# The inverse stage in float32 on quarters of the array, and spectra of batch 1 held back behind it

## The chip, the cores and the metric

One core of one Trainium2 chip runs the kernel. The time is that of the device, in microseconds, from one launch. Only TensorE multiplies matrices; VectorE, ScalarE and GpSimd work element by element; SyncE (SP) and the other engines' queues start DMAs. An engine takes its instructions in the order in which they stand in its list and waits at each for what it needs.

## The reference

The input x is 4 batches of 3072 tokens with 256 channels. Three layers follow one another:

```python
X = np.fft.rfft(x, axis=1)                       # over the tokens of a batch
Yr = Xr @ w_r - Xi @ w_i + b_r;  Yi = Xr @ w_i + Xi @ w_r + b_i
Y = soft_threshold(Yr, 0.01) + 1j * soft_threshold(Yi, 0.01)
x = np.fft.irfft(Y, n=3072, axis=1)              # 12288 tokens in all
e = argmax(x @ w_gate)                           # one of 8 experts
# in token order the first 384 tokens of an expert are kept, the rest give 0
y = gate_weight * (relu(x @ w1[e]) @ w2[e])
out = silu(y @ w_in) @ w_out                     # for the kept tokens
```

Since an expert keeps its first 384 tokens only, the kernel transforms batch 0 and the beginning of batch 1, and takes a second, longer way through all batches only where an expert is not full by then. That way is not run with these inputs.

## The kernel before, in words

The transform over 3072 tokens is done in factors of 48 and 64. For a batch `s1` multiplies by a 96 x 96 table (tile `c1f`) and writes to a scratch array `a_d`. `kphase` then runs over k = 0, 2, ..., 22, two frequencies at a time: `forward` reads rows `ar` and makes the spectrum (tile `xp`, the products that the order calls `xp<-c,ar`, then copies and differences `xk`), `shrink` multiplies by the weights (24 float32r products `yp<-wri,xk`) and applies the threshold on VectorE (`y`, `cl`, `cl`), and `back` transforms back (`bp<-cl,c`) and writes to a scratch array `b_d`. For one k, `shrink` comes one step and `back` three steps later. A float32 operand is split into a high and a low float32r part, and three float32r products (`mm3`: high by high, low by high, high by low) give nearly the float32 result.

The inverse stage `is2` reads `b_d` in 8 groups g (rows `br`), splits each row tile into `bh` and `bl`, multiplies by `c4`, copies to `ao`, writes `attn`, turns `ao` by transposes (`tp`, copied to `aT`), and multiplies by the gate's weights (`lg<-aT,wg`); after groups 3 and 7 the logits are turned (`lt`) and `choose` picks experts. `route` counts positions with VectorE passes and two small products (`bs`), makes the one-hot factors `ft` and matrices `pm`, and multiplies them (`tb<-ft,pm`) into a table of token numbers and gate weights. `rank` orders the experts by load (`key`, `rk`, `sel`, `ids`, `idi`); SP reads `idi` to load the weights (`st`) of the first experts, and `slots` makes the addresses `srcs` with which GpSimd gathers the tokens `xg`. Those are scaled by VectorE, turned (`gtp`) and split (`xT`), and then the experts' layers begin (`hp`, `y`, `h`, `o`) and run to the end; beside the first of them `third` does the inverse stage, the gate and the routing for the first third of batch 1 (`ps<-br,c4p`).

A planner with estimated costs puts each engine's list in order ahead of the run: an instruction that is written later may be moved up where its inputs would be ready. So spectra of batch 1 (`self.kphase(1, ads, True)`, written behind `is2`, `route` and `rank`) stand among the inverse stage of batch 0. `after(ins, first)` adds a wish of order to that planner: `ins` stands behind `first` on the same engine, with no semaphore. Tiles with one tag share that tag's buffers, and in PSUM, which has 8 banks, `ps` has three of them, `xp` two, and `yp`, `yq` and `bp` one each; `lg` of `is2` uses the bank `yq`.

Of the kernel before, what the change touches and what calls it, by code (L numbers as in the profile page):

```python
# [17 lines left out]
N1, N2 = 48, 64  # L18
# [18 lines left out]
HELD = 10  # L37
FULL = 0, 1, 3, 5, 7, 9, 11, 13, 15
BIG = 65536.0
UP = 65536.0  # L40
# [10 lines left out]
def _split(a):  # L51
    hi = _round12(a)
    return hi, _round12(a - hi.astype(np.float64))


def _tables():
# [23 lines left out]
    c1 = np.einsum("akr,pz->apkrz", c1, eye2).reshape(Q, Q)  # L80
    c4 = np.einsum("kra,pz->krpaz", c4, eye2).reshape(Q, Q)
    m = np.zeros((NK, 2, N2, 2, N2))
# [10 lines left out]
    for half, f0 in ((0, 0), (1, N1 // 2)):  # L93
# [22 lines left out]
    ind = ind.transpose(1, 0, 2).reshape(2, 2 * P)  # L116
    u, q = np.arange(P) // QB, np.arange(P) % QB
    at = TW * q + GT * u
# [3 lines left out]
        "c1": np.stack(_split(c1) + (c1,), 1).reshape(Q, -1),  # L122
        "c4": np.stack(_split(c4) + (c4,), 1).reshape(Q, -1),
        "tab": tab,
# [28 lines left out]
class Kernel:  # L153
    def __init__(self, ctx, tc, i, o):
# [17 lines left out]
        self.stored = {}  # L172
        self.again, self.evicted = False, None

# [208 lines left out]
    def kphase(self, b, ads, ahead=False):  # L383
# [12 lines left out]
        def spectrum(xp, ar, kq, tb):  # L396

            for c in range(2):
                nc.tensor.matmul(xp[:, c], ar[:, kq, c * P:(c + 1) * P], c2[:, tb], start=True, stop=True)

        def forward(k, ar):
            first = k == 0
            kq = k % KG
            xk = kp.tile([P, 2, 4, 192], FR, tag="xk", name="xk", bufs=3)
            xp = self.pk.tile([P, 4, P], F32, tag="xp", name="xp", bufs=self.xb)
            for j in range(2):
                spectrum(xp[:, 2 * j:2 * j + 2], ar, kq + j, k + j + 1)
            js = slice(2, 4) if first else slice(0, 4)
            up, mid, low = slice(64, 192), slice(128, 192), slice(0, 64)
            nc.scalar.copy(xk[:, 0, :, up], xp)  # L410
            v.tensor_tensor(xk[:, 1, :, up], xp, raw(xk[:, 0, :, up]), ALU.subtract)
            nc.scalar.activation(xk[:, 0, js, low], xp[:, js, 64:], AF.Copy, scale=-1.0)
            v.tensor_tensor(xk[:, 1, js, low], raw(xk[:, 0, js, mid]), xp[:, js, 64:], ALU.subtract)
            xo = None
            if first:
                xp = self.pk.tile([P, 4, P], F32, tag="xp", name="xp", bufs=self.xb)
                spectrum(xp, ar, 0, 0)
                xo = kp.tile([P, 2, 2, P], FR, name="xo", bufs=1)
                self.split("av", xo[:, 0], xo[:, 1], xp[:, :2])
            return xk, xo  # L420

        def shrink(k, xk, xo):
            yp = self.pk.tile([P, 2, D], F32, tag="yq" if k % 4 and b != 1 else "yp", name="yp", bufs=1)
            for j in range(2):
# [41 lines left out]
    def route_consts(self):  # L466
        nc, bp = self.nc, self.bc
        self.c4 = bp.tile([Q, 2, Q], FR, name="c4", bufs=1)
        t = bp.tile([Q, 3, Q], F32, name="c4f", bufs=1)
        nc.sync.dma_start(out=t, in_=self.i["c4"].rearrange("q (h m) -> q h m", h=3))  # L470
        nc.vector.tensor_copy(self.c4, t[:, 0:2])
        self.c4p = bp.tile([Q, QB], F32, name="c4p", bufs=1)
        nc.vector.tensor_copy(self.c4p, t[:, 2, 0:QB])
        kw = dict(allow_small_or_imprecise_dtypes=True)
# [38 lines left out]
    def third(self, b, res):  # L513

        nc, bp, ps, wg, CH = self.nc, self.bp, self.ps, self.wg, self.CH
        v = nc.vector
        c4 = self.c4p
        bv = self.bds[b].rearrange("k (r u g) c -> (k r) u (g c)", r=4, u=4)
        od = self.attn[0][b * S:b * S + QB * TW].rearrange("(q u g) d -> u q (g d)", u=4, g=GT)
        res[b] = self.chosen(1)  # L520
        def rows(n):
# [10 lines left out]
            for u in range(4):  # L532
                nc.sync.dma_start(out=od[u, :, n * CH:(n + 1) * CH], in_=aof[u * QB:(u + 1) * QB])
            return ao
# [29 lines left out]
    def is2(self, b, qbs, res):  # L564
# [3 lines left out]

        nc, bp, ps, c4, wg, CH, LD = self.nc, self.bp, self.ps, self.c4, self.wg, self.CH, self.LD
        v = nc.vector  # L570
        NB = len(qbs)
        q0, nq = qbs[0] * QB, NB * QB
        qs = slice(q0, q0 + nq)
        bv = self.bds[b].rearrange("k (r u g) c -> (k r) u g c", r=4, u=4)
        r0 = b * S + q0 * TW
        h = int(r0 >= NEAR)
        od = self.attn[h][r0 - h * NEAR:r0 - h * NEAR + nq * TW].rearrange("(q u g) d -> q u g d", u=4, g=GT)
        res[b] = self.chosen(NB)
# [3 lines left out]
        def rows(g):  # L582
            br = bp.tile([Q, LD], F32, tag="xt", name="br", bufs=self.sb)
            nc.sync.dma_start(out=br.rearrange("q (u c) -> q u c", c=D), in_=bv[:, :, g])
            ao = bp.tile([Q, 4, 2, P], F32, tag="ao", name="ao2", bufs=self.sb)
            aof = ao.rearrange("q u h d -> q (u h d)")
            for z in range(0, LD, CH):
                sl = slice(z, z + CH)
                bh = bp.tile([Q, CH], FR, tag="xh", name="bh", bufs=self.sb)
                bl = bp.tile([Q, CH], FR, tag="xl", name="bl", bufs=self.sb)  # L590
                self.split("av", bh, bl, br[:, sl])
                pt = ps.tile([Q, CH], F32, tag="ps", name="ps2")
                self.mm3(pt[:nq], c4[:, 0, qs], c4[:, 1, qs], bh, bl, True, True)
                nc.scalar.copy(aof[:nq, sl], pt[:nq])
            nc.scalar.dma_start(out=od[:, :, g], in_=aof[:nq].rearrange("q (u c) -> q u c", c=D))
            return ao

        def turn(ao):
            aT = bp.tile([P, 2, NB, 4, QB], F32, tag="aT", name="aT")
            for h in range(2):  # L600
                tp = ps.tile([P, 4, nq], F32, tag="ps", name="tp")
                for u in range(4):
                    nc.tensor.transpose(tp[:, u], ao[:nq, u, h], self.ident[:nq, :nq])
                v.tensor_copy(aT[:, h].rearrange("p b u q -> p u b q"), tp.rearrange("p u (b q) -> p u b q", q=QB))
            return aT

        def gate(g, aT):
# [4 lines left out]
            for h in range(2):  # L612
                for j in range(NB):
                    nc.tensor.matmul(lg[COL * j:COL * (j + 1), z], wg[:, h], aT[:, h, j].rearrange("p u q -> p (u q)"),
                                     start=h == 0, stop=h == 1)
            if z == GS - 1:
# [18 lines left out]
    def route(self, b, qbs, res):  # L635
# [466 lines left out]
```

## Time and profile before

| | |
|---|---|
| three runs | 655.97, 658.72, 662.19 us, median 658.72 |
| profiled execution | 661.11 us, its span 659.3 us |
| mean granted TensorE clock | 0.967 |
| TensorE busy | 623.8 us, 95% of the span |
| DMA | 83.1 MB, 126 GB/s over the span |

The profile is of one execution. Times of its rows count from the span's start. A TensorE row gives the start, the duration, the source line and the product, with its shape; one float32 product is recorded twice, so that x2 is one product, and a float32r product once. Durations of products overlap, so what a row of products costs is the distance from start to start. The granted clock is a share of 2.4 GHz; 0.50 is 1.2 GHz.

### The profile page before, as it was taken

Reading aid. Unit: us, or ns where it says so; the run is one execution under the profiler, and the core shown is the slowest. Engines: PE = TensorE matmul, PEld = TensorE weight load, DVE = VectorE, ACT = ScalarE, POOL = GpSimd, SP = SyncE. Lnnn points to the kernel's source line nnn. Section 1 sums busy time; section 2 is a strip of 40 time slices with the busy share of each in tenths; the row PEclk is TensorE's granted clock in tenths of the full one; section 3 lists DMA queues with packets and bytes.
Section 4 is the critical chain, followed back from the end, with each engine's and each line's share of the span. In section 5 each row is a group of like instructions: output and inputs, shape, how many; then the busy total and the mean of one; then the engine's idle time right before and its main releaser. Section 6 shows DMA issues by size and latency. Waiting matters only on the chain. (4 is left out here: it accounts for less than half of the span.)

```text
span 659.3 us, 10829 instructions
## 1 busy us (share of the span) xinstructions
PE 623.8 (95%) x4060; PEld 570.1 (86%) x4060; DVE 331.8 (50%) x673; ACT 314.8 (48%) x640; POOL 76.6 (12%) x81
## 2 busy tenths in 40 slices
PE   8699999999985999999999999999999999999993
PEld 4387889877873579899999999999999999999993
DVE  3348986667595579973423236632225632223330
ACT  4434543555331356654645445544544554544450
POOL 1001220000013211250101022000112000101001
PEclk9779999999995899999999999999999999999998
DMA  8996945893217865799600014400004400000000
GB/s 240 320 242 195 302 167 162 211 275 106 81 64 212 267 203 160 224 322 345 194 9 17 9 34 150 129 17 1 25 9 122 126 18 1 25 1 25 1 1 29
DMA packets 63542, 83.10 MB, mean 126 GB/s; under 512 B 4948, under 2 KB 53144, under 8 KB 63480
## 3 DMA queue, kind: packets, MB, share of 16 engines
q1 hardware_dynamic: 51640, 66.58, 33.3%
q10 hardware_dynamic: 9536, 9.44, 4.6%
q0 software_dynamic: 2304, 6.29, 3.0%
q8 instruction: 34, 0.56, 0.3%
q14 instruction: 28, 0.23, 0.1%
HBM read 49.79 MB, written 32.51 MB: 125 GB/s over the span
## 5 line engine op out<-in xcount | busy, mean ns | idle before, releaser
L190 DVE TENSOR_TENSOR gl<-sg,gh 128x384 fp32r<-128x384 f32 x118 | 65.5, 558 | 160.9 <-ACT gh L182 157.2
L1025 ACT ACTIVATE sg<-h 128x384 f32<-128x384 f32 x128 | 62.6, 492 | 112.2 <-PE h L200 111.4
L199 PE MATMUL o<-wo,gl 128*128 128x256 f32 x354 | 92.9, 282 | 0.0
L200 PE MATMUL o<-wo,gh 128*128 128x256 f32 x354 | 92.8, 282 | 0.0
L198 PE MATMUL h<-yT,wi 128*128 128x384 f32 x256 | 86.3, 337 | 0.4 <-ACT yT L182 0.4
L199 PE MATMUL h<-yT,wi 128*128 128x384 f32 x256 | 86.1, 336 | 0.0
L200 PE MATMUL h<-yT,wi 128*128 128x384 f32 x256 | 85.7, 337 | 0.0
L198 PE MATMUL o<-wo,gh 128*128 128x256 f32 x354 | 73.6, 282 | 0.0
L199 PEld LDWEIGHTS o<-wo,gl 128*128 128x128 f32 x354 | 67.1, 189 | 0.1
L200 PEld LDWEIGHTS o<-wo,gh 128*128 128x128 f32 x354 | 67.1, 190 | 0.0
L182 ACT CAST gh<-sg 128x384 fp32r<-128x384 f32 x118 | 60.2, 514 | 8.7 <-PE o L200 5.7
L198 PEld LDWEIGHTS o<-wo,gh 128*128 128x128 f32 x354 | 59.9, 189 | 0.0
L182 ACT CAST w<-st 128x512 fp32r<-128x512 f32 x64 | 39.2, 619 | 36.5 <-DMA st<-in_moe_w 17.9
L198 PE MATMUL yp<-wri,xk 128*128 128x256 f32 x188 | 55.2, 293 | 0.0
L190 DVE TENSOR_TENSOR w<-st,w 128x512 fp32r<-128x512 f32 x64 | 45.7, 718 | 17.9 <-ACT w L182 17.8
L199 PE MATMUL yp<-wri,xk 128*128 128x256 f32 x188 | 54.3, 289 | 0.0
L200 PE MATMUL yp<-wri,xk 128*128 128x256 f32 x188 | 53.5, 285 | 0.0
L991 ACT ACTIVATE hh<-hp 128x384 fp32r<-128x384 f32 x64 | 31.5, 492 | 41.3 <-PE y L199 19.9
L198 PEld LDWEIGHTS h<-yT,wi 128*128 128x128 f32 x256 | 48.2, 188 | 0.7 <-ACT yT L182 0.7
L199 PEld LDWEIGHTS h<-yT,wi 128*128 128x128 f32 x256 | 48.1, 188 | 0.0
L200 PEld LDWEIGHTS h<-yT,wi 128*128 128x128 f32 x256 | 48.1, 188 | 0.0
L992 DVE SCALAR_TENSOR_TENSOR hl<-hp,hh 128x384 fp32r<-128x384 f32 x64 | 35.1, 552 | 24.6 <-ACT hh L991 24.4
(224 smaller groups left out, 1255.2 us busy)
## 6 DMA issues: line engine op xcount, KB each, us to landing
st<-in_moe_w SPq DMA_DIRECT2D x64, 256.0 KB, 3.4
out<-zt SPq DMA_DIRECT2D x48, 256.0 KB, 3.6
a_d<-ao SPq DMA_DIRECT2D x16, 384.0 KB, 4.9
ar<-a_d SPq DMA_DIRECT2D x12, 512.0 KB, 5.1
b_d<-bo ACTq DMA_DIRECT2D x12, 512.0 KB, 3.0
br<-b_d SPq DMA_DIRECT2D x16, 384.0 KB, 4.7
xt<-in_x SPq DMA_DIRECT2D x15, 384.0 KB, 6.9
nt<-in_moe_w_in SPq DMA_DIRECT2D x8, 512.0 KB, 7.9
```

Source lines behind the costliest of these rows:

```text
L182: self.nc.scalar.copy(dst, src)
L190: e.tensor_tensor(dst, src, raw(hi), ALU.subtract)
L198: first = nc.tensor.matmul(out, lh, rh, start=start, stop=False)
L199: nc.tensor.matmul(out, ll, rh, start=False, stop=False)
L200: return first.ins, nc.tensor.matmul(out, lh, rl, start=False, stop=stop).ins
L991: nc.scalar.activation(hh, hp, AF.Relu)
L992: self.evicted = nc.vector.scalar_tensor_tensor(hl, hp, 0.0, raw(hh), ALU.max, ALU.subtract).ins
L1025: nc.scalar.activation(sg, hp, AF.Silu)
```

## The change

`c4` is now one float32 table: a 48 x 48 table in the partitions 0 to 47 and once more in 64 to 111, and the third's table behind it. `tiled` multiplies the two halves of the rows (parity p, 48 partitions each) by it in float32, for two column halves ch, into four quarters of the array: rows 64p, output partitions 64ch. It takes two PSUM banks, one for each p. The token order inside a group changes with it: partition and free index swap roles, so reads and writes are made of two DMAs each, `third` and the token numbers follow, and transposes are 128 wide. `gated[g]` keeps the last gate product of group g; spectra of batch 1 for k = 8 are put behind group 2, k = 10 behind group 5, and k = 12 to 22 behind group 7. In batch 1 the products `yp` for k = 14, 18 and 22 use the bank `yq`. One factor of `route` moves from GpSimd to VectorE.

```diff
+PACE = {4: 2, 5: 5, **{n: GT - 1 for n in range(6, 12)}}
...
+    def tiled(self, table, rows, pool):
+        out = [pool.tile([P, self.CH], F32, tag="ps", name="ps1") for _ in range(2)]
+        for ch in range(2):
+            for p in range(2):
+                at = slice(64 * p, 64 * p + N1)
+                self.nc.tensor.matmul(out[p][64 * ch:64 * ch + 64], table[at, :64], rows[at, ch * self.CH:(ch + 1) * self.CH],
+                                      start=True, stop=True)
+        return out
...
         def forward(k, ar):
...
+            behind = self.gated[PACE[k // 2]] if b == 1 and k // 2 in PACE else None
             for j in range(2):
-                spectrum(xp[:, 2 * j:2 * j + 2], ar, kq + j, k + j + 1)
+                for ins in spectrum(xp[:, 2 * j:2 * j + 2], ar, kq + j, k + j + 1):
+                    if behind:
+                        self.after(ins, behind)
...
-            yp = self.pk.tile([P, 2, D], F32, tag="yq" if k % 4 and b != 1 else "yp", name="yp", bufs=1)
+            yp = self.pk.tile([P, 2, D], F32, tag="yq" if k % 4 and (b != 1 or k > 12) else "yp", name="yp", bufs=1)
...
         def rows(g):
-            br = bp.tile([Q, LD], F32, tag="xt", name="br", bufs=self.sb)
-            nc.sync.dma_start(out=br.rearrange("q (u c) -> q u c", c=D), in_=bv[:, :, g])
-            ao = bp.tile([Q, 4, 2, P], F32, tag="ao", name="ao2", bufs=self.sb)
-            aof = ao.rearrange("q u h d -> q (u h d)")
-            for z in range(0, LD, CH):
-                sl = slice(z, z + CH)
-                bh = bp.tile([Q, CH], FR, tag="xh", name="bh", bufs=self.sb)
-                bl = bp.tile([Q, CH], FR, tag="xl", name="bl", bufs=self.sb)
-                self.split("av", bh, bl, br[:, sl])
-                pt = ps.tile([Q, CH], F32, tag="ps", name="ps2")
-                self.mm3(pt[:nq], c4[:, 0, qs], c4[:, 1, qs], bh, bl, True, True)
-                nc.scalar.copy(aof[:nq, sl], pt[:nq])
-            nc.scalar.dma_start(out=od[:, :, g], in_=aof[:nq].rearrange("q (u c) -> q u c", c=D))
+            br = bp.tile([P, 4, D], F32, tag="xt", name="br", bufs=self.sb)
+            for p in range(2):
+                nc.sync.dma_start(out=br[64 * p:64 * p + N1], in_=bv[p, :, :, g])
+            pt = self.tiled(self.c4, br.rearrange("q u c -> q (u c)"), ps)
+            ao = bp.tile([P, 2, 2, D], F32, tag="ao", name="ao2", bufs=self.sb)
+            for p in range(2):
+                nc.scalar.copy(ao[:, p].rearrange("q u c -> q (u c)"), pt[p])
+            for ch in range(2):
+                nc.scalar.dma_start(out=od[:, :, 2 * ch:2 * ch + 2, g], in_=ao[64 * ch + t0:64 * ch + t0 + nt])
...
-        nc.gpsimd.tensor_tensor(ft[:, :, 0], mk, tok.to_broadcast(sh), ALU.mult)
+        v.tensor_tensor(ft[:, :, 0], mk, tok.to_broadcast(sh), ALU.mult)
```

Three places of the engines' lists show the move. First TensorE in the inverse stage, from the third group on. Before, the list read (`c_1037` is the table `c4`):

```order
L399 MATMUL xp<-c_241,ar 128x128 x4
L198 MATMUL ps_1129<-bh,c_1037 96x512
L199 MATMUL ps_1129<-bh,c_1037 96x512
L200 MATMUL ps_1129<-bl,c_1037 96x512
L198 MATMUL ps_1138<-bh,c_1037 96x512
L199 MATMUL ps_1138<-bh,c_1037 96x512
L200 MATMUL ps_1138<-bl,c_1037 96x512
L614 MATMUL lg<-aT,wg 32x128 x3
L603 MATMUL tp<-ident,ao_1089 128x96 x4
L614 MATMUL lg<-aT,wg 32x128 x3
L198 MATMUL yp<-wri,xk 128x256
```

and 12 of the products `yp` follow. Now it reads:

```order
L358 MATMUL ps_1107<-br,c_1037 64x512 x2
L358 MATMUL ps_1108<-br,c_1037 64x512 x2
L629 MATMUL lg<-aT,wg 32x128 x3
L462 MATMUL bp<-cl,c_242 128x256 x2
L616 MATMUL tp<-ident,ao_1084 128x128 x4
L629 MATMUL lg<-aT,wg 32x128 x3
L616 MATMUL tp<-ident,ao_1084 128x128 x4
L358 MATMUL ps_1143<-br,c_1037 64x512 x2
L358 MATMUL ps_1144<-br,c_1037 64x512 x2
L629 MATMUL lg<-aT,wg 32x128 x3
L616 MATMUL tp<-ident,ao_1113 128x128 x4
L629 MATMUL lg<-aT,wg 32x128 x3
```

From the third group to the sixth only one pair `bp` and one spectrum `xp` stand between the groups. In the whole stage 55 products `yp` are left, where 136 stood between its first product and its last gate before.

Second, TensorE around the route's table product. Before:

```order
L443 MATMUL bp<-cl,c_242 128x256 x4
L707 MATMUL tb<-ft,pm 128x72 x24
L528 MATMUL ps_2276<-br,c4p 32x512 x4
L973 MATMUL gtp<-ident,xg 128x128 x2
L528 MATMUL ps_2321<-br,c4p 32x512 x2
```

and now, where 24 products `yp` with one pair `bp` among them stand in place of the line that is left out:

```order
L462 MATMUL bp<-cl,c_242 128x256 x2
L721 MATMUL tb<-ft,pm 128x72 x24
...
L462 MATMUL bp<-cl,c_242 128x256 x4
L987 MATMUL gtp<-ident,xg 128x128 x6
L205 MATMUL hp<-xT,w_2114 128x384
```

The last step of batch 1's spectra has moved behind the table product, and the third's products behind the first expert's.

Third, VectorE behind the matrices `pm` that this product needs. Before, the ranking stands together and the table and the addresses follow:

```order
L734 TENSOR_REDUCE ids<-big 128x8
L736 CAST idi<-ids 128x8
L738 TENSOR_TENSOR big<-sel,carry 128x24
L739 TENSOR_REDUCE least<-big 128x3
L929 TENSOR_REDUCE low<-least 1x1
L710 TENSOR_TENSOR table<-table,tb 128x72
L753 TENSOR_TENSOR tmps<-table,sel 128x216
L755 TENSOR_REDUCE ents<-tmps 128x27
```

and now:

```order
L432 TENSOR_TENSOR xk<-xk,xp 128x4x64
L453 TENSOR_TENSOR y<-yp,bias 128x512
L746 TENSOR_TENSOR big<-sel,col 128x64
L724 TENSOR_TENSOR table<-table,tb 128x72
L455 TENSOR_SCALAR cl<-y 128x512
L748 TENSOR_REDUCE ids<-big 128x8
L767 TENSOR_TENSOR tmps<-table,sel 128x216
L456 TENSOR_TENSOR cl<-y,cl 128x512
L750 CAST idi<-ids 128x8
```

Passes of the spectra now stand between those of the ranking, the table and the addresses, and `idi` comes behind the table.

## Rows read from the trace of the kernel before

**Rows 1.** The page: busy us, share and instructions of each engine.

```profile
PE 623.8 (95%) x4060; PEld 570.1 (86%) x4060; DVE 331.8 (50%) x673; ACT 314.8 (48%) x640; POOL 76.6 (12%) x81
```

**Rows 2.** Windows: stretch, length, engines' busy us (instructions), clock, DMA share, GB/s.

```profile
124.50:178.60 54.10, 52.64 (x419) 42.35 (x417) 36.28 (x72) 27.43 (x55) 0.00 (x0) 1.00 0.60 170
...
196.00:199.10 3.10, 0.01 (x1) 0.04 (x1) 3.10 (x4) 2.06 (x5) 1.20 (x1) 0.98 0.34 116
199.10:219.40 20.30, 14.24 (x48) 7.35 (x48) 9.44 (x30) 3.38 (x6) 6.22 (x6) 0.50 0.79 243
...
sum 96.40, PE 84.42 PEld 65.12 DVE 63.50 ACT 39.80 POOL 8.49; mean PE 16.88 PEld 13.02 DVE 12.70 ACT 7.96 POOL 1.70
```

**Rows 3.** Timeline of TensorE in the inverse stage: start, us, line, product, shape.

```profile
134.03 1.03 PE L443 MATMUL bp<-cl,c 128*128 128x256 f32 x4
134.89 1.05 PE L399 MATMUL xp<-c,ar 128*128 128x128 f32 x8
135.70 0.48 PE L198 MATMUL ps<-bh,c 96*96 96x512 f32 x1
136.02 0.40 PE L199 MATMUL ps<-bh,c 96*96 96x512 f32 x1
136.25 0.39 PE L200 MATMUL ps<-bl,c 96*96 96x512 f32 x1
...
137.62 0.55 PE L603 MATMUL tp<-ident,ao 96*128 96x96 f32 x4
138.10 0.42 PE L614 MATMUL lg<-aT,wg 128*32 128x128 f32 x6
138.45 0.38 PE L198 MATMUL yp<-wri,xk 128*128 128x256 f32 x1
138.67 0.28 PE L199 MATMUL yp<-wri,xk 128*128 128x256 f32 x1
138.79 0.28 PE L200 MATMUL yp<-wri,xk 128*128 128x256 f32 x1
```

**Rows 4.** Chain of waits: start, us, what; three 128-wide transposes.

```profile
507.00 0.33 PE gtp L973 x3
```

**Rows 5.** Timeline of TensorE: a float32 product alone, and two on column strips.

```profile
15.25 1.02 PE L372 MATMUL ps<-xt,c1f 96*96 96x512 f32 x2
...
224.38 1.05 PE L528 MATMUL ps<-br,c4p 96*32 96x512 f32 x4
```

**Rows 6.** Timeline of TensorE: the last gate, the table product, the first expert product.

```profile
178.15 0.42 PE L614 MATMUL lg<-aT,wg 128*32 128x128 f32 x6
...
199.09 5.31 PE L707 MATMUL tb<-ft,pm 128*128 128x72 f32 x24 [3.13 <-DVE pm L695]
...
220.79 0.45 PE L198 MATMUL hp<-xT,w 128*128 128x384 f32 x1
```

**Rows 7.** Timeline of VectorE from the last spectra to the addresses.

```profile
192.84 0.69 DVE L434 TENSOR_TENSOR y<-yp,bias 128x512 f32<-128x512 f32 x1
...
197.74 2.35 DVE L695 TENSOR_TENSOR pm<-iota,r 128x1024 fp32r<-128x1024 f32 x2
...
201.48 0.17 DVE L736 CAST idi<-ids 128x8 int32<-128x8 f32 x1
...
204.44 0.23 DVE L710 TENSOR_TENSOR table<-table,tb 128x72 f32<-128x72 f32 x1 [2.31 <-PE tb L707]
...
205.76 0.16 DVE L760 CAST srcs<-slas 128x9 int32<-128x9 f32 x1
```

**Rows 8.** Timelines of GpSimd, VectorE, ScalarE: gathers, scaling, first cast of weights.

```profile
206.89 1.21 POOL L961 DMA_INDIRECT xg<-attn,srcs  x1 [9.69 <-DMA br<-b_d]
...
209.72 1.00 POOL L961 DMA_INDIRECT xg<-attn,srcs  x1 [0.30 <-issue]
...
214.49 0.60 DVE L965 TENSOR_SCALAR xg<-xg,gws 128x256 f32<-128x256 f32 x2
...
209.57 0.62 ACT L182 CAST w<-st 128x512 fp32r<-128x512 f32 x1 [11.51 <-DMA st<-in_moe_w]
```

More of the change, by code (lines that the diff above doesn't have):

```diff
@@ L80, in _tables, with halves @@
     c1 = np.einsum("akr,pz->apkrz", c1, eye2).reshape(Q, Q)
-    c4 = np.einsum("kra,pz->krpaz", c4, eye2).reshape(Q, Q)
+    third = np.einsum("kra,pz->krpza", c4[:, :, :QB // 2], np.eye(2)).reshape(Q, QB)
+    def halves(t):
+        t = np.pad(t.reshape(N1, N1), ((0, 64 - N1), (0, 64 - N1)))
+        return np.concatenate([t, t])
+    c4 = np.concatenate([halves(c4), np.pad(third, ((0, P - Q), (0, 0)))], axis=1)
     m = np.zeros((NK, 2, N2, 2, N2))
@@ L122, in _tables @@
         "c1": np.stack(_split(c1) + (c1,), 1).reshape(Q, -1),
-        "c4": np.stack(_split(c4) + (c4,), 1).reshape(Q, -1),
+        "c4": c4,
         "tab": tab,
@@ L172, in __init__ @@
         self.stored = {}
-        self.again, self.evicted = False, None
+        self.again, self.evicted, self.gated = False, None, {}
     def after(self, ins, first):
@@ L396, in spectrum @@
         def spectrum(xp, ar, kq, tb):
-            for c in range(2):
-                nc.tensor.matmul(xp[:, c], ar[:, kq, c * P:(c + 1) * P], c2[:, tb], start=True, stop=True)
+            return [nc.tensor.matmul(xp[:, c], ar[:, kq, c * P:(c + 1) * P], c2[:, tb], start=True, stop=True).ins for c in range(2)]
         def forward(k, ar):
@@ L467, in route_consts @@
         nc, bp = self.nc, self.bc
[L468 to L473, printed above, removed]
+        self.c4 = bp.tile([P, 64 + QB], F32, name="c4", bufs=1)
+        nc.sync.dma_start(out=self.c4, in_=self.i["c4"])
         kw = dict(allow_small_or_imprecise_dtypes=True)
@@ L516, in third @@
         v = nc.vector
-        c4 = self.c4p
+        c4 = self.c4[:Q, 64:]
         bv = self.bds[b].rearrange("k (r u g) c -> (k r) u (g c)", r=4, u=4)
-        od = self.attn[0][b * S:b * S + QB * TW].rearrange("(q u g) d -> u q (g d)", u=4, g=GT)
+        od = self.attn[0][b * S:b * S + QB * TW].rearrange("(t p u g) d -> u p t (g d)", p=2, u=4, g=GT)
         res[b] = self.chosen(1)
@@ L532, in rows @@
             for u in range(4):
-                nc.sync.dma_start(out=od[u, :, n * CH:(n + 1) * CH], in_=aof[u * QB:(u + 1) * QB])
+                for p in range(2):
+                    at = u * QB + p * (QB // 2)
+                    nc.sync.dma_start(out=od[u, p, :, n * CH:(n + 1) * CH], in_=aof[at:at + QB // 2])
             return ao
@@ L564, in is2 @@
     def is2(self, b, qbs, res):
-        nc, bp, ps, c4, wg, CH, LD = self.nc, self.bp, self.ps, self.c4, self.wg, self.CH, self.LD
+        nc, bp, ps, wg = self.nc, self.bp, self.ps, self.wg
         v = nc.vector
         NB = len(qbs)
[L572 to L575, printed above, removed]
+        T = QB // 2
+        t0, nt = qbs[0] * T, NB * T
+        bv = self.bds[b].rearrange("k (r p u g) c -> p (k r) u g c", r=2, p=2, u=4)
+        r0 = b * S + t0 * 2 * TW
         h = int(r0 >= NEAR)
-        od = self.attn[h][r0 - h * NEAR:r0 - h * NEAR + nq * TW].rearrange("(q u g) d -> q u g d", u=4, g=GT)
+        od = self.attn[h][r0 - h * NEAR:r0 - h * NEAR + nt * 2 * TW].rearrange("(t p u g) d -> t p u g d", p=2, u=4, g=GT)
         res[b] = self.chosen(NB)
@@ L595, in rows @@
-            nc.scalar.dma_start(out=od[:, :, g], in_=aof[:nq].rearrange("q (u c) -> q u c", c=D))
+            br = bp.tile([P, 4, D], F32, tag="xt", name="br", bufs=self.sb)
[3 more added lines that the diff above has]
+            ao = bp.tile([P, 2, 2, D], F32, tag="ao", name="ao2", bufs=self.sb)
+            for p in range(2):
+                nc.scalar.copy(ao[:, p].rearrange("q u c -> q (u c)"), pt[p])
@@ L596, in rows @@
+            for ch in range(2):
+                nc.scalar.dma_start(out=od[:, :, 2 * ch:2 * ch + 2, g], in_=ao[64 * ch + t0:64 * ch + t0 + nt])
             return ao
         def turn(ao):
-            aT = bp.tile([P, 2, NB, 4, QB], F32, tag="aT", name="aT")
+            aT = bp.tile([P, 2, NB, P], F32, tag="aT", name="aT")
             for h in range(2):
[L601 to L604, printed above, removed]
+                tp = ps.tile([P, 4, P], F32, tag="ps", name="tp")
+                for x in range(4):
+                    nc.tensor.transpose(tp[:, x], ao[:, x % 2, x // 2, h * P:(h + 1) * P], self.ident)
+                for ch in range(2):
+                    v.tensor_copy(aT[:, h].rearrange("c b (o x t) -> c o b x t", o=2, x=4)[:, ch],
+                                  tp.rearrange("c x (o b t) -> c o b x t", o=2, t=T)[:, ch, qbs[0]:qbs[0] + NB])
```

5 lines of the change are left out of this document (2 added, 3 removed).

## The prediction

> **What bounds the kernel now.** The page's busy line comes first [rows 1]: TensorE is busy 623.8 of 659.3 us, no other engine over 332. The change can pay only by shortening TensorE's own list or by giving back time in which TensorE stands or runs slow. The windows say where that time is [rows 2]. The stretch of the change runs from the first product of the inverse stage (124.5) to the first expert product (220.8, [rows 6]). There TensorE is busy 84.42 of 96.4 us, so 12.0 us are idle; in the stretch 199.1 to 219.4 the granted clock is 0.50, so half of its 14.24 busy us, 7.1, is lost too. Together **19.1 us**; the work itself, at the full clock, is 77.3 us. Most of the loss lies after 196: the spectra of batch 1 are used up, while the routing of batch 0 still runs on VectorE, then the table, the gathers and the reads of batch 1. One idle stretch of 3.1 us (196.0 to 199.1) was enough for the clock to be at 0.50 after it.
>
> So the change is sound in aim: keep spectra back, and they fill the routing. The question is what it costs ahead of that, and how long the chain behind the routing still is when the last spectrum is done.
>
> **Prices on TensorE** [rows 3]. In a run of spectra a float32r product of 256 columns starts 0.12 us after the one ahead of it (138.67, 138.79), but 0.22 passes where float32 products stood before (138.45, 138.67): a switch costs 0.10. A back transform's pair takes 0.86 (134.03 to 134.89), four spectrum products 0.81 (134.89 to 135.70), three gate products 0.35 (138.10 to 138.45), four 96-wide transposes about 0.4 (137.62 to 138.10, switch included). One 128-wide transpose takes 0.11 [rows 4].
>
> **Part 1, the inverse stage's products.** Out: 8 groups x 6 float32r products; one in a row takes 0.23 (136.02, 136.25, [rows 3]), so 8 x 6 x 0.23 = 11.0 us. In: 8 groups x 4 float32 products of 512 columns on quarters. A float32 product of 512 columns alone takes 1.02 with its end, and two of them on different column strips together 1.05 [rows 5]: strips run side by side. That two halves of the rows do so too no row shows. Bounds for a group: 0.95 if all four run together (0.87 of streaming, 1.02 less its end, and a switch), 1.75 if only the two columns do. I take 0.95, because the column pair behaved so. The first two groups are cut in halves by other work, which adds about 0.9 each. 8 x 0.95 + 1.8 = 9.4, so this part gains 1.6; with serial rows it would lose 4.8.
>
> The Trainium skill ("TensorE: Matmul & The Clock Gate", Part 3) says that small matmuls on distinct row and column groups run concurrently, and gives 3.07x for four row tiles; with it a group is 0.95, as I took it.
>
> **Part 2, transposes.** 64 transposes of 128 columns for 64 of 96: by columns 0.11 against 0.083 (an estimate from [rows 4]), 1.7 us more. Splits leave ScalarE (8 x 2 casts) and VectorE (8 x 2 subtractions); neither was the bound there, so I count nothing. Each group's two copies stay on ScalarE, and its DMAs double in number (48 partitions each, same bytes); the DMA share in 124.5 to 178.6 is 0.60 [rows 2], and now the reads of the 16 halves stand in SP's queue with nothing between, so I count nothing for them either.
>
> **Part 3, the switches.** With fewer spectra between its parts, the stage changes from one kind of product to another about as often as before. Rows put 0.10 on each, and the net is 0.
>
> The Trainium skill ("TensorEngine Tiling (Array Packing)", Tiling Modes) states that changing the tiling mode drains the engine, which speaks against quarters between full-width transposes. If some 40 changes each cost the 0.16 between a product's 0.28 and its pitch of 0.12 [rows 3] and not 0.10, the stage would be 2.4 us longer.
>
> **Part 4, what moves.** 8 spectrum products that stood ahead of 121.6 now come after the stage (+1.6 us of work); in their place TensorE runs spectra and then waits for the first rows, which come no earlier. Inside the stage PSUM's three banks of the small pool turn over faster (two for the products, two for a transpose), bounds 0 to 4 us, since there is little else to run; I take 1.
>
> The order shows where the last gate falls: 55 spectra products, 8 spectrum products and 4 pairs are left inside the stage, so it ends after 9.4 (products) + 7.0 (transposes) + 5.6 (16 triples of gates) + 6.6 + 1.6 + 3.4 + 5.4 (40 switches, the banks' 1.0, the first half's logits 0.4) = 39.0 us after 124.2, at about **163** (before: 178.5, [rows 6]).
>
> **Part 5, the new gap.** From that gate to the route's table product there are 137 spectra products (16.4), six forward transforms (4.9), four pairs (3.4), 1.3 of small ones and 1.2 of switches: 27 us, to about 190. VectorE's list up to the end of the matrices took 21.6 before (178.5 to 200.1, [rows 6, 7]), with four shrink steps and the two passes of one spectrum in it; now it has four shrink steps and five spectra, so 4 x 2 passes of up to 0.69 more, about 4.5, and less waiting: 23 to 26, so that TensorE is the later one. The three factors cost it nothing net: three passes in place of two, of which one ran beside GpSimd's. So the table product starts at about 190, runs at the full clock for 2.65 (half of 5.31, [rows 6]) and ends at E = 192.7. What is left then for TensorE: 24 spectra products and three pairs, **5.6 us**.
>
> The chain from E: before, the table was updated right after the product (204.44), and the gather's addresses stood at 205.94, 1.5 later [rows 7]. Now, as the order shows, VectorE has shrink and spectrum passes of up to 0.69 each [rows 7] ahead of the table and between it and the addresses, and the ranking, which ran under the product before, too. From the end of the matrices to the table that is about 4.7, so 1.6 after E, and 3.1 more to the addresses: E + 4.7 against 1.5. Then the gathers: the first is issued 0.95 after the addresses, the third 2.8 later [rows 8], and the third tile was scaled at 215.1, 9.15 after the addresses; DMAs were near full then (0.79), so I take 8.5. Transposes, casts and the subtraction that stands behind the weights' on VectorE: 2.5. The weights themselves are cast a few us after SP reads the ranking (201.65 to 209.57 before, [rows 7, 8], with reads of batch 1 in front that now come later), ahead of the gathers. First expert product: E + 15.7. So TensorE's gap is 15.7 - 5.6 - 0.7 (the transposes) = **9.4 us**. Bounds: 5 (gathers land in 3.5 and VectorE runs ahead of its order) and 12. After such a gap the clock is at 0.50, as at 199.1; before it needed from 214 to 219.4 to come back. Of that stretch some 3.5 us are expert products now: 1.8 lost.
>
> **Sum**, against the profiled execution (661.11 us, span 659.3): -19.1 (all old losses) - 1.6 + 1.7 + 1.6 + 1.0 + 9.4 + 1.8 = -5.2. The products of batch 1's third that ran ahead of 220.8 are in the 77.3 and still have to run, so they need no term. 661.1 - 5.2 = 655.9. The median of the runs shown is 658.7, 2.4 under the profiled one, so I forecast **653.5**, 0.8% less.
>
> **The rivals.**
> - *Faster, 647, chance 0.27.* The gap is 5, and, since a pair of back transforms falls into it, the clock holds: 6.2 us better. For it: other gathers land in less, and reads of batch 1 no longer stand ahead of the weights in SP's queue. Against: the in-order list of VectorE.
> - *Rows of the array run one after the other, 660, chance 0.11.* The stage is 8 x 0.8 = 6.4 us longer, TensorE bound all the way. Against: columns do overlap [rows 5].
> - *The first experts wait, 658.5, chance 0.10.* Loads that had the old idle stretch to themselves (weights, reads of batch 1, gathers) must now come beside the first expert; SP also issues 32 stores of the third in place of 16. 5 us of stalls. Against: even in 199.1 to 219.4, when all of them ran, the DMA share was 0.79, not 1 [rows 2].
> - *Slower, 666, chance 0.10.* The clock falls inside the inverse stage. From the third group to the sixth, some 13 us, TensorE has almost nothing but quarter products, 32-column gates and transposes; the stage before always had spectra between them at clock 1.00 [rows 2]. At 0.50 these 13 us become up to 26. It decides if the clock falls before the spectra after the sixth group: 653.5 + 12.5 = 666. Against: in 214 to 219.4 transposes and column pairs of the third, and no spectra, were what ran before the clock rose again [rows 2, 5].
>
> **How the numbers follow.** The forecast has 0.42, with its own range of 650 to 658. About 1%, 6.6 us, is what a measurement of this kernel can tell from no change (its three runs lie within 6.2). Faster by more, under 652.1: the first rival and a third of the forecast, 0.40. Slower by more: the last rival and the far end of the loads, 0.12. Within: 0.48. Range 645 to 662: it takes in both middle rivals and most of the first, and leaves out the last.
>
> **What would show it.** Inverse stage right: the last gate of batch 0 at 161 to 166, clock 1.00, groups of four quarter products in about 1.0. Serial rows: 1.75. Routing covered: no idle TensorE and clock 1.00 from there to the table product at about 190. The gap: addresses 4 to 5 us after the table product, TensorE idle some 9 us and a clock of 0.50 before the first expert product, at 207 to 211. The forecast is wrong if that product starts before 204, if TensorE stands in the stage for more than 5 us, or if it waits for loads in the first two experts.

## The result and the profile after

The change takes 651.77 us in the median of 20 runs (649.12 to 656.8), against 657.95 of the kernel before beside it (20 runs, 653.49 to 662.19): a ratio of **0.9916, 95% interval 0.9896 to 0.9935** (the ratio is not the quotient of the two medians). That is 6.2 us less by the medians and 5.5 by the ratio. The forecast was 653.5 with a range of 645 to 662. The profiled execution has a span of 651.8 (before 659.3) and a mean clock of 0.980 (before 0.967).

The page of the profile after, its line of engines, answers to [rows 1]: TensorE is busy 7.3 us less.

```profile
PE 616.5 (95%) x4076; PEld 563.4 (86%) x4076; DVE 320.3 (49%) x673; ACT 306.1 (47%) x624; POOL 75.4 (12%) x79
```

The windows of after by stage answer to [rows 2]: from the first product of the inverse stage to the last gate, from there to the table product, from there to the first expert product; columns as there.

```profile
122.60:158.80 36.20, 36.20 (x312) 23.10 (x311) 18.35 (x53) 13.78 (x26) 0.00 (x0) 1.00 0.79 199
158.80:185.50 26.70, 26.70 (x220) 26.09 (x219) 23.21 (x62) 12.39 (x27) 0.00 (x0) 1.00 0.32 107
185.50:202.90 17.40, 11.56 (x69) 9.30 (x67) 11.53 (x37) 5.85 (x12) 6.29 (x7) 0.79 0.61 180
```

TensorE does not stand for a moment in the first two stretches, at the full clock. All that is left of the old loss lies in the third: 5.8 us idle, and a clock of 0.79.

TensorE's timeline of after: the start of the stage, two groups of quarter products among gates and transposes ([rows 3, 5] before), then the steps of [rows 6].

```profile
122.60 1.07 PE L358 MATMUL ps<-br,c 48*64 48x512 f32 x4
123.60 1.13 PE L462 MATMUL bp<-cl,c 128*128 128x256 f32 x4
...
135.49 1.09 PE L358 MATMUL ps<-br,c 48*64 48x512 f32 x8
136.50 0.42 PE L629 MATMUL lg<-aT,wg 128*32 128x128 f32 x6
136.85 0.66 PE L616 MATMUL tp<-ident,ao 128*128 128x128 f32 x4
137.44 0.42 PE L629 MATMUL lg<-aT,wg 128*32 128x128 f32 x6
137.79 0.66 PE L616 MATMUL tp<-ident,ao 128*128 128x128 f32 x4
138.38 1.09 PE L358 MATMUL ps<-br,c 48*64 48x512 f32 x8
139.40 0.42 PE L629 MATMUL lg<-aT,wg 128*32 128x128 f32 x6
...
158.79 0.42 PE L629 MATMUL lg<-aT,wg 128*32 128x128 f32 x6
...
185.53 2.95 PE L721 MATMUL tb<-ft,pm 128*128 128x72 f32 x24
...
196.71 2.08 PE L462 MATMUL bp<-cl,c 128*128 128x256 f32 x4 [3.55 <-ACT bo L189]
...
200.97 0.69 PE L987 MATMUL gtp<-ident,xg 128*128 128x128 f32 x2 [1.76 <-DVE xg L979]
...
202.87 0.69 PE L205 MATMUL hp<-xT,w 128*128 128x384 f32 x1 [0.35 <-ACT xT L189]
```

The eight records are four float32 products of 512 columns (a transpose, unlike them, is recorded once). From 138.38 to the next product they take 1.02, and with their end 1.09, where one such product alone takes 1.02 with its end [rows 5]. The last gate comes 19.4 us earlier than before, the table product 13.6, the first expert product 17.9.

VectorE's timeline of after answers to [rows 7].

```profile
181.77 2.36 DVE L709 TENSOR_TENSOR pm<-iota,r 128x1024 fp32r<-128x1024 f32 x2
...
187.16 0.69 DVE L453 TENSOR_TENSOR y<-yp,bias 128x512 f32<-128x512 f32 x1
...
188.52 0.23 DVE L724 TENSOR_TENSOR table<-table,tb 128x72 f32<-128x72 f32 x1 [0.55 <-PE tb L721]
...
190.88 0.15 DVE L774 CAST srcs<-slas 128x9 int32<-128x9 f32 x1
```

Of the 17.9 us by which the experts start earlier, 10.4 are given back behind that point: from the first expert product to the end of the span it is 448.9 us now (651.8 less 202.9) and was 438.5 (659.3 less 220.8). Some of this is only moved: before, four groups of the third's products ran ahead of the first expert product, as the prediction says in its sum. Much of the rest is seen in the windows of the 72 us from the first expert product on, first of the kernel before, then of after.

```profile
220.80:292.80 72.00, 70.89 (x407) 61.66 (x408) 62.99 (x152) 43.08 (x86) 17.96 (x15) 1.00 0.71 221
```

```profile
202.90:274.90 72.00, 65.20 (x363) 54.01 (x364) 51.68 (x125) 35.67 (x74) 13.15 (x10) 0.96 0.75 220
```

TensorE stands 6.8 us there, against 1.1. The waits of TensorE in that stretch of after (us in total, times, longest):

```profile
PE y L205 <- ACT hh L1005: 4.7, 2, 3.0
PE ps L543 <- DMA br<-b_d: 2.1, 3, 0.9
```

The longest of them, by the timelines of TensorE, ScalarE and SP's queue in after:

```profile
247.19 0.69 PE L205 MATMUL y<-hh,w 128*128 128x384 f32 x1 [3.01 <-ACT hh L1005]
...
246.09 0.66 ACT L833 ACTIVATE na<-nt 128x512 f32<-128x512 f32 x1 [3.92 <-DMA nt<-in_moe_w_out]
...
234.71 5.13 SPq L550 DMA_DIRECT2D attn<-ao  x8
...
242.30 0.94 SPq L827 DMA_DIRECT2D nt<-in_moe_w_out  x2
```

In this place the activation `hh` stands on ScalarE behind the first pass `na` on a piece of a weight, that pass waits 3.92 for its load, and the load was issued behind eight stores of the third, which alone kept SP's queue 5.13 us. So three suspects: the doubled stores, the pass on ScalarE, and the order as a whole. And a larger question: which of the four parts of the change (the quarters, the ties of the spectra behind the gates, the late banks, the factor moved to VectorE) brings the gain?

### The profile page after: what moved, and what is told of

Its sections match the earlier page's. It is cut to its first block, busy times and chain, and to the rows that moved or that the text cites. A ratio compares the mean times of both kernels' runs of the same rounds, so it can differ in the third digit from the quotient of the medians.

```text
span 651.8 us, 10889 instructions
## 1 busy us (share of the span) xinstructions
PE 616.5 (95%) x4076; PEld 563.4 (86%) x4076; DVE 320.3 (49%) x673; ACT 306.1 (47%) x624; POOL 75.4 (12%) x79
## 5 line engine op out<-in xcount | busy, mean ns | idle before, releaser
L205 PE MATMUL y<-hh,w 128*128 128x384 f32 x128 | 45.1, 352 | 4.7 <-ACT hh L1005 4.7
L1005 ACT ACTIVATE hh<-hp 128x384 fp32r<-128x384 f32 x64 | 31.2, 490 | 36.3 <-PE y L206 17.6
```

What stands on the lines that cost most here:

```text
L205: first = nc.tensor.matmul(out, lh, rh, start=start, stop=False)
L1005: nc.scalar.activation(hh, hp, AF.Relu)
```

## The experiments

Each ran in 5 rounds beside the kernel before, whose medians were 656.84 to 657.85. "Start" is the first expert product, "stage" the time from the first product of the inverse stage to the last gate, "busy" TensorE's busy time in the 72 us from the start on. The last three columns are of one profiled execution each. The runs were made on several chips, so kernels are better compared by their ratios than by their times.

| kernel | us | ratio to before, 95% interval | stage | start | busy |
|---|---|---|---|---|---|
| before | 657.95 | 1 | 52.9 | 220.8 | 70.9 |
| the change | 651.77 | 0.9916 (0.9896 to 0.9935) | 36.2 | 202.9 | 65.2 |
| e1: no ties | 664.98 | 1.0118 (1.0078 to 1.0158) | 56.4 | 217.7 | 68.6 |
| e2: ties, late banks, no quarters | 649.33 | 0.9867 (0.9834 to 0.99) | 35.5 | 201.9 | 70.0 |
| e3: no late banks | 648.15 | 0.9835 (0.9795 to 0.9874) | 36.2 | 198.8 | 68.8 |
| e12: e3 again | 650.79 | 0.9886 (0.9851 to 0.992) | 36.2 | 198.9 | 69.9 |
| e7: ties alone | 650.72 | 0.9881 (0.9841 to 0.9922) | 35.5 | 201.2 | 71.6 |
| e4: stores from ScalarE | 658.86 | 1.002 (0.9998 to 1.0043) | 36.2 | 201.3 | 61.7 |
| e5: 16 stores | 654.31 | 0.9952 (0.9923 to 0.9982) | 36.2 | 200.2 | 66.3 |
| e6: no late banks, 16 stores | 652.98 | 0.9927 (0.9895 to 0.996) | 36.3 | 199.0 | 64.5 |
| e8: the change, gap filled | 649.64 | 0.9892 (0.9846 to 0.9939) | 36.4 | 200.0 | 68.1 |
| e9: pass off ScalarE | 651.07 | 0.9909 (0.9881 to 0.9937) | 36.2 | 201.1 | 66.3 |
| e10: e3, gap filled | 652.18 | 0.9927 (0.9901 to 0.9952) | 36.2 | 203.3 | 68.5 |
| e11: e2, gap filled | 650.61 | 0.991 (0.9881 to 0.9938) | 36.7 | 204.4 | 70.5 |

### e1: the change without the ties

```diff
-PACE = {4: 2, 5: 5, **{n: GT - 1 for n in range(6, 12)}}
+PACE = {}
```

> The quarters and the late banks stay, the ties of batch 1's spectra are taken away. Theory A (the ties give the gain: spectra fill the routing, so that the first expert product comes at 203 and not at 212 to 220): the spectra run out before the table product again, TensorE idles more than 10 us between it and the first expert product, and the time goes back to 656 to 660. Theory B (the shorter inverse stage gives the gain, TensorE's list decides): the time stays at 650 to 653.

1.2% slower than before: what theory A says of the idle time holds (11.9 us between the table product and the first expert product), but the time lies 5 us above its range. TensorE's timeline of this kernel, last gate, table product, first transposes of tokens, first expert product:

```profile
178.02 0.42 PE L629 MATMUL lg<-aT,wg 128*32 128x128 f32 x6
...
198.94 2.87 PE L721 MATMUL tb<-ft,pm 128*128 128x72 f32 x24
...
213.18 0.69 PE L987 MATMUL gtp<-ident,xg 128*128 128x128 f32 x2 [9.20 <-DVE xg L979]
...
217.66 0.69 PE L205 MATMUL hp<-xT,w 128*128 128x384 f32 x1 [1.98 <-ACT xT L189]
```

The gate and the table product stand where they stood before [rows 6], and the idle stretch is back. Why it is even slower than before, though its first expert product starts 3.1 us earlier, no run shows. The timelines suggest one reason: the last pair of batch 1 comes later here (202.04, before 194.87), so that its store is issued at 208.24 (before 197.14), and the third's first product falls from 207.58, inside the gap, to 223.36, behind it. Quarters, late banks and the moved factor by themselves bring nothing.

### e2: ties and late banks, with the old inverse stage

The edit is the kernel before with the change's lines on `PACE`, `gated`, `behind` and `tag="yq"`, and none of `tiled`; the factor of `route` stays on GpSimd.

> The kernel before with the ties and the late banks, but with its three float32r products, splits and layout. Theory A: most of the gain is there, 652 to 656; the stage takes some 3 to 6 us longer than with quarters, because its products are 11.0 us and not 8.2, and because its chain (cast, subtraction, product, copy) has little else to run beside it. Theory B: no gain, 657 to 660.

At least as fast as the change (the two intervals overlap at their ends, 0.9896 to 0.99), and faster than theory A's range, which had the stage 3 to 6 us longer than with quarters. The timeline of TensorE in this kernel:

```profile
121.59 1.03 PE L446 MATMUL bp<-cl,c 128*128 128x256 f32 x4
...
123.07 0.47 PE L199 MATMUL ps<-bh,c 96*96 96x512 f32 x1 [0.46 <-ACT bh L183]
...
158.56 0.64 PE L617 MATMUL lg<-aT,wg 128*32 128x128 f32 x12
...
184.84 0.98 PE L710 MATMUL tb<-ft,pm 128*128 128x72 f32 x8
...
201.93 0.69 PE L199 MATMUL hp<-xT,w 128*128 128x384 f32 x1 [0.99 <-ACT xT L183]
```

and its windows, the stage and the first 72 us of the experts:

```profile
123.10:158.60 35.50, 35.33 (x286) 26.08 (x288) 26.21 (x53) 21.28 (x41) 0.00 (x0) 1.00 0.66 194
```

```profile
201.90:273.90 72.00, 69.99 (x389) 58.31 (x390) 57.26 (x132) 38.46 (x78) 13.84 (x10) 0.96 0.81 245
```

The stage with its split rows and three products each is 0.7 us shorter than the one on quarters. But the two do not hold the same work: a pair of back transforms that stands inside the change's stage (123.60) stands ahead of this one (121.59), and a pair costs 0.9 to 1.1 (0.86 in [rows 3]). Without it the two stages are within 0.4 us: what the products save, the wider transposes and the switches cost. The start comes 0.9 earlier than in the change, and behind it TensorE stands 2.0 us in place of 6.8. The whole gain is there without quarters.

### e3 and e12: the change without the late banks, twice

```diff
-            yp = ... tag="yq" if k % 4 and (b != 1 or k > 12) else "yp" ...
+            yp = ... tag="yq" if k % 4 and b != 1 else "yp" ...
```

> All of the change, but the products of batch 1's shrink steps keep to one bank to the end. Theory A with the banks as a part of it: each of the last five shrink steps waits for VectorE to read the bank ahead of it, which in the new order stands behind passes of the route; up to 0.7 us each, so 653 to 655, with idle time of TensorE before the table product that the changed kernel has not. Rival: a transform and a pair stand between two shrink steps (1.7 us) and cover it, 651 to 653.

Faster than the change and below both ranges; of the waits that theory A names, 0.5 us of idle time ahead of the table product came. TensorE's timeline:

```profile
157.33 0.42 PE L629 MATMUL lg<-aT,wg 128*32 128x128 f32 x6
...
181.65 2.88 PE L721 MATMUL tb<-ft,pm 128*128 128x72 f32 x24
...
198.75 0.69 PE L205 MATMUL hp<-xT,w 128*128 128x384 f32 x1 [0.35 <-ACT xT L189]
```

The order can explain the time, though no run shows that it does: with one bank for batch 1, the planner puts the table product ahead of two shrink steps and not of one: 24.3 us behind the last gate in place of 26.7. That leaves 48 spectra products and not 24 to run beside the chain of addresses and gathers. The same kernel once more:

> The change with the bank rule of before once more, word for word the kernel that gave 648.15. Theory A (the order with the early table product is better by some 3.5 us): 646.5 to 649.5, a ratio to before of 0.983 to 0.988. Theory B (kernels of this family differ by 2 to 3 us from one build or chip to the next, and that run was a lucky one): 650 to 653, a ratio of 0.990 to 0.994.

650.79: the time lies in theory B's range, the ratio of 0.9886 between the two, and its interval overlaps that of the first run; the two together are around 0.986. The order is the same in both, and both starts lie below that of the change (198.8 and 198.9). Against the change the two runs are 3.6 and 1.0 us less by the medians, 5 and 2 by the ratios, and the interval of the second overlaps that of the change. So dropping the late banks probably helps with quarters, by an amount that these runs leave open.

### e7: the kernel before with the ties alone

The edit is e2 with the bank rule of before.

> The kernel before with the ties alone: neither quarters nor two late banks. Theory A (the late banks cost because with them the planner places the route's table product behind more shrink steps): the same gain as in the change, 3 us or more, against the ties with the late banks (649.3), so 645 to 647, with the table product starting earlier than 184.8. Theory B (the one bank helped only together with quarters): 649 to 650.

The table product starts at 182.86 (24.6 behind the last gate), as theory A says, but the time is theory B's: 650.72. From the table product to the first expert product it takes 18.3 us here and 17.1 in e2, which gives most of it back. With e7 the gain stands on the ties alone. Between e2, e3, e12 and e7 no run tells a better one: their intervals all overlap.

### e4, e5, e6: the third's stores

e4 issues the 32 stores from ScalarE's queue, e5 and e6 make 16 of them, with one more dimension each; e6 has the bank rule of before as well.

```diff
-                for p in range(2):
-                    at = u * QB + p * (QB // 2)
-                    nc.sync.dma_start(out=od[u, p, :, n * CH:(n + 1) * CH], in_=aof[at:at + QB // 2])
+                nc.sync.dma_start(out=od[u, :, :, n * CH:(n + 1) * CH], in_=aof[u * QB:(u + 1) * QB])
```

> The 32 stores of the third go out from ScalarE's queue, not from SP's. In the changed kernel TensorE idles 6.8 us between 210 and 275, 3.0 of it behind a ReLU that stands on ScalarE behind a load of w_out, which SP issued behind 8 stores that it had waited for. Theory C (SP's queue with twice the stores is the cause): that wait goes, the idle time falls to 2 to 4 us and the time to 646 to 649. Rival D (the DMAs themselves are late, since all loads now come beside the first experts): the load of w_out and the reads of batch 1 land as late as before, and the time is 650 to 653.

> The change, with the third's rows stored by 16 transfers from SP's queue instead of 32. Theory A (the waits in the first experts come from the doubled stores, which stand in SP's queue ahead of the loads of the weights of the reducing experts): those waits, some 4 us, go, and the time is 647 to 649; the wait of the activation on its load falls from 3.9 us to under 1. Theory B (the waits come from the order of the instructions after the gap: the third's products and the experts' tiles stand differently, and VectorE and ScalarE are late): under 1 us of difference, 651 to 653.

> The change, with the bank rule of the kernel before (three shrink steps in four of batch 1 in the other bank: no, all of batch 1 in one) and 16 stores. Theory A: the gain of the one bank (3.6 us) and that of the stores (3 to 4) add: 644 to 646. Theory B: the one bank's gain alone, 647.5 to 649.

None was faster, and all three times lie above both of their ranges. By their intervals e4 is slower than the change and e6 slower than e3 (though not than e12), while e5 is level with the change. In e4 the load behind the stores is no longer late (`na` waits 1.8 us for its loads in place of 10.3), but ScalarE now waits in its own list; from 202 to 275 it waits longest for TensorE, and 3.9 us for stores to give their buffer back (us in total, times, longest):

```profile
ACT w L189 <- PE hp L207: 10.7, 6, 4.5
...
ACT ao L546 <- DMA attn<-ao: 3.9, 1, 3.9
```

TensorE is busy 61.7 of 72 us, and 7 us are lost against the change. In e5 SP's queue spends half as long on a chunk's stores, by its timeline:

```profile
232.02 2.57 SPq L548 DMA_DIRECT2D attn<-ao  x4
```

but the pass `na` still waits up to 4.8 for its load, where theory A had under 1, TensorE still stands 5.7 us in its first 72, and the time is 654.31. So halving the time that the stores keep SP's queue brings nothing: the theories that rest on it fall.

### e9: the pass on the weight's pieces off ScalarE

```diff
-        nc.scalar.activation(a, high, AF.Abs, scale=UP)
+        if src[0][0].shape[-1] == D:
+            nc.gpsimd.tensor_scalar(a, high, UP, None, ALU.mult)
+            v.tensor_scalar(u, u, 0x7FFFFFFF, None, ALU.bitwise_and)
+        else:
+            nc.scalar.activation(a, high, AF.Abs, scale=UP)
```

> The change, with the first pass on each loaded piece of the second feed-forward weight (absolute value and scale) taken from ScalarE: GpSimd scales, VectorE clears the sign. That pass waited 10.3 us for loads in the first experts, and an activation on which TensorE waited 3.0 us stood behind it. Theory A (the loads block ScalarE, and with it TensorE): the waits of TensorE on the activation hh there fall from 4.7 us to under 1, and the time is 647 to 649. Theory B (TensorE waits for whatever stands late in the new order, and another wait takes its place): 650 to 653.

The time is theory B's. TensorE's waits in the first 72 us of its experts:

```profile
PE hp L207 <- DVE xT L197: 2.2, 1, 2.2
PE ps L543 <- DMA br<-b_d: 1.5, 1, 1.5
PE hp L205 <- ACT xT L189: 1.4, 1, 1.4
PE y L207 <- DVE hl L1010: 1.4, 2, 0.8
```

The wait on `hh`, 4.7 us of it, is gone, and nearly as much stands at other places (TensorE stands 5.7 us in place of 6.8); the time is the same. Removing the longest single wait did not shorten the whole.

### e8, e10, e11: products of zeros in the gap

```diff
+            if b == 1 and k == NK - 2:
+                self.fill(24)
             bp = self.pk.tile([P, 2, D], F32, tag="bp", name="bp", bufs=1)
...
             self.hi("a", bo[:, k % KG:k % KG + 2], bp)
+            if b == 1 and k == NK - 2:
+                self.fill(12)
```

`fill(n)` issues n float32r products of 256 columns of a tile of zeros into a PSUM tile that nothing reads.

> The change, with 24 products of zeros before the last pair of back transforms and 12 after it, where TensorE stood for some 5 us. They add 4.3 us of work in idle time. Theory A (the half clock after the gap costs about 2 us): the granted clock stays at 1.00 up to some 198 and falls less or not at all after it, and the time is 649 to 650.5. Theory B (the half clock lies on idle time and costs under 0.7): 651 to 652.5. If the products of zeros delay the first expert product, the time is above 653.

> The change with the bank rule of before, and with products of zeros in the gap (24 ahead of the last pair, 12 behind it). Theory A (they add: the order with the early table product, and the clock): 645.5 to 647.5. Theory B (in this order the clock was down for only a short while, at 0.80 and 0.85, so there is little to hold): 647.5 to 649.

> The kernel before with ties and late banks, without quarters, and with the products of zeros in the gap, where the clock was at 0.50 to 0.79 for some 12 us. Theory A (the clock costs about 2 us whatever the inverse stage is): 647 to 648 with a clock of 1.00 from 190 to 210. Theory B (the fill's effect in the change was another order of the first experts, not the clock): 649 to 650.5.

In e8 the clock held. Its windows:

```profile
195.00:200.00 5.00, 3.52 (x22) 2.75 (x22) 3.53 (x9) 3.10 (x7) 2.69 (x4) 1.00 1.00 307
200.00:205.00 5.00, 4.67 (x25) 4.34 (x26) 3.02 (x8) 2.02 (x5) 3.02 (x3) 1.00 0.91 283
```

against these of the change:

```profile
195.00:200.00 5.00, 2.50 (x6) 1.64 (x6) 1.69 (x4) 2.80 (x6) 3.79 (x4) 0.56 1.04 324
200.00:205.00 5.00, 3.50 (x11) 2.53 (x12) 4.66 (x11) 2.51 (x5) 1.90 (x2) 0.50 0.88 278
```

e8 gains 2.1 us by the medians and 1.6 by the ratios, within theory A's range, but its interval overlaps that of the change. In e8 the zeros delay nothing (table product to first expert product 16.3 us, in the change 17.3), but the planner has also set the first experts in another order, with 0.4 us of the wait on `hh` in place of 4.7. In e10 and e11 the zeros came too late and stood in the way; TensorE's timeline of e10:

```profile
194.50 3.22 PE L300 MATMUL pf<-zr 128*128 128x256 f32 x24
199.88 1.10 PE L472 MATMUL bp<-cl,c 128*128 128x256 f32 x4 [2.16 <-DVE cl L464]
200.63 1.78 PE L300 MATMUL pf<-zr 128*128 128x256 f32 x12
202.25 0.82 PE L999 MATMUL gtp<-ident,xg 128*128 128x128 f32 x6
203.31 0.45 PE L205 MATMUL hp<-xT,w 128*128 128x384 f32 x1 [0.24 <-ACT xT L189]
```

The first expert product lies 21.7 us behind the table product, 4.6 more than in e3, where the last pair stands behind the first expert products (201.82) and not ahead of the transposes. The clock was at 1.00 from 190 on in e10, and from 200 on in e11 (0.66 from 195 to 200); with the later start neither got faster, and both times lie above their two ranges (e11 by 0.1). So the price of the half clock, 1.8 us in the prediction, is not shown by a time: e8 fits 2 us, and no run excludes less. By the windows of the change, TensorE runs 2.8 us of expert products at 0.50 (202.9 to 205.7), of which half, 1.4, is lost.

## Why the prediction was right, and where it was not

**The aim.** Right: keeping spectra back fills the routing. From the end of the last gate to the table product 27 us were forecast and 26.3 came, without idle time, at a clock of 1.00. And this is the whole gain: e2 and e7 have it without quarters, e1 loses it.

**The inverse stage.** Right in kind, 2.4 us too long: 39.0 forecast, 36.6 measured to the end of the last gate, which came at 159.2 in place of 163 and ahead of the 161 to 166 that the prediction names (1.6 of these 4.0 lie ahead of the stage, which began at 122.6 and not 124.2; over all profiles of this case it began between 120.0 and 125.2). In the kernel before its first product starts at 125.23; at 124.5, which the prediction takes for it, a pair of back transforms starts. All four quarters run together, 1.02 a group where 0.95 was taken and 1.75 was the bound, so the rival with serial rows falls. The Trainium skill's rule that small matmuls on distinct row and column groups run concurrently ("TensorE: Matmul & The Clock Gate", Part 3) is borne out by that row. The 1.0 us for PSUM's banks did not come: TensorE was busy 36.20 of 36.20. The switches cost less than 0.10 each: from 135.49 to 138.38 a whole group takes 2.89, 8 such groups 23.1, and the prediction's terms for them, without spectra and cut groups, add up to 24.2 (7.6 for the quarters, 7.0, 5.6, 4.0). The drain that the Trainium skill states for a change of tiling mode ("TensorEngine Tiling (Array Packing)", Tiling Modes) would have added 2.4 us by the prediction's estimate; the rows show less than the sum without it. The rival in which the clock falls in the stage did not come about: 1.00 from 122.6 to 195.

**The quarters' worth.** The prediction put it at 1.6 less 1.7, so nothing, and that is what e2 against the change shows for the stage (35.5 and 36.2, with one pair more in the latter). TensorE is busy throughout in both (36.20 of 36.20 and 35.33 of 35.50), so the sum of its products decides, and the relief of ScalarE and VectorE buys nothing here.

**The gap.** The chain behind the table product was mis-sized at one step. The table's update came right after the product (188.52), and the addresses stood at 191.03 (190.88 and 0.15), 2.5 us after the product's end at 188.48, not 4.7: the passes that stand ahead of the table in VectorE's list ran under the product (the last threshold from 187.16), where 1.6 us of them had been counted behind it, and from the table to the addresses it was 2.5 and not 3.1. From the addresses to the first expert product 11.0 were forecast (8.5 and 2.5) and 11.8 came. So the first expert product started at 202.9. The prediction had named "before 204" as a sign that its forecast is wrong; together with the earlier stage that is 5.5 us better than its 208.4. The gap itself had 5.8 us of idle time, not 9.4 and close to the bound of 5, and the clock fell all the same, to 0.50 from 200 to 205. Most of the 5.8 us, 3.55, lies ahead of the last pair, whose bank ScalarE empties late: its copy `bo` (196.08) stands behind a cast of weights that waited 4.67 for its load (195.55).

**The first experts.** This is the step that failed on the other side. The rival "the first experts wait" was priced at 5 us and given 0.10; it came, with 5.7 us more idle time than before in 72 us. Its reason, loads that must come beside the experts, is only half seen: TensorE waited for `hh` behind a load, but stores taken out of SP's queue (e4) or halved in it (e5) and the pass taken off ScalarE (e9) moved the waits and did not remove them. The planner sets where the first experts' tiles and the third's products stand, and in e5, e8 and e9 they stand in another order than in the change. TensorE is busy 61.7 to 71.6 of those 72 us over the rows of the table, and the same order twice (e3, e12) gave 68.8 and 69.9. The kernels with the old inverse stage have 70.0 to 71.6, those with quarters 61.7 to 69.9. One wait comes with the quarters in every profile: that of the third's products on the rows they read (`ps` on `br`), 0.4 to 3.7 us in the ten kernels with quarters and 0.2 at most in the four with the old stage. No run takes it away, and why quarters come with more idle time there, though the third's products are the same, stays open.

**The total.** 5.5 us better at the start of the experts, 3.2 worse behind it (448.9, by the prediction's terms 445.7): 2.3 us better than its sum of 654.1 for the span, and 1.7 below the forecast median. By the windows of both kernels, the 10.4 us that are given back behind the start are 4.9 of idle time over the whole rest (5.7 more in the first 72 us, 0.8 less after them), 1.4 of half clock and 4.2 of work that only moved, where the prediction had 0, 1.8 and 5.4. So the time came out near the forecast by errors of opposite sign: the start too late, the stalls behind it left out of the sum. That they nearly cancel is luck, though a bound and a rival had named both.

## What to carry to other kernels

In a change of several parts, time each part alone: here one dictionary that ties spectra behind the gates brings the whole gain, and the rewritten stage, most of the diff, brings none. Price a stage that TensorE fills without a pause by the sum of its products, and look whether the two stages that you compare hold the same work. Here relieving the engines beside it brought nothing. Where a planner orders the lists, an edit also shuffles what comes behind it: TensorE's idle time in the first experts lies between 0.4 and 10.3 us in these kernels. And the same kernel, in the same order, gave 648.15 and 650.79 us, so a difference of 2 or 3 us between two such kernels is not yet the worth of the edit.

## What was not expected of the hardware

- Four float32 products of 512 columns on four quarters, rows and columns apart, take 1.09 us together with their end, hardly more than one alone (1.02 in [rows 5]).
- A store of 16 partitions kept SP's queue as long as one of 32 partitions with one more dimension: 0.64 us each in the rows shown (8 in 5.13 and 4 in 2.57), 0.42 to 0.87 and 0.58 to 0.68 over all rows of the two kernels (the change and e5). In the kernel before a store of 32 partitions kept it 0.31 to 0.52.
- Removing a wait of 3.92 us on ScalarE, and the wait of TensorE behind it, left the time where it was (e9).
